# 288 instead of 320 columns of scores for a key block: a quarter of the own block shares columns with the far block

## The chip, the cores and the metric

One Trainium2 chip, and one of its cores. The metric is device microseconds of one execution. The kernel has five instruction streams: PE (matmuls, with the weight loads shown apart as PEld), ACT (exponentials and copies), DVE and POOL (elementwise work), and SP, which issues DMAs. Streams run in order and wait for each other by semaphores.

## The reference, cut to what matters

Four layers follow each other on `x` of 2048 tokens by 512 features, each with a layer norm ahead and a residual behind. Layers 1 and 3 are linear attention (`A`), layers 2 and 4 are attention in a sliding window (`B`). Both have 32 heads of 16 features.

```python
def _B_ref(x, wqkv, wo):
    H = 32; Dh = D // H; W = 256
    q, k, v = ...                       # x @ wqkv, split in heads
    scores = jnp.einsum("bhqd,bhkd->bhqk", q, k) * (Dh ** -0.5)
    mask = (idx[:, None] - idx[None, :] >= 0) & (idx[:, None] - idx[None, :] < W)
    p = _softmax(jnp.where(mask, scores, -1e9), axis=-1)
    return heads_joined(einsum("bhqk,bhkd->bhqd", p, v)) @ wo
x = x + _A_ref(_layernorm(x), A_wqkv, A_wo)
x = x + _B_ref(_layernorm(x), B_wqkv, B_wo)
x = x + _A_ref(_layernorm(x), A_wqkv, A_wo)
x = x + _B_ref(_layernorm(x), B_wqkv, B_wo)
```

A key k is seen by the 256 queries k to k + 255. A block of 64 keys is therefore seen by 320 queries: its own 64 (where the query must not be before the key), 192 that see all its keys, and 64 far ones (where the query must be less than 256 behind the key). A query offset r of the own part sees keys up to r; the far query with the same offset sees keys above r. So together the two parts hold 64 queries' worth of scores in 128 columns.

## The kernel before

**Tiles.** Tokens come in 16 tiles (or blocks) of 128, numbered j; half-blocks b of 64 keys. `kB` holds keys with two heads side by side: 64 keys by 2 heads are 128 columns of weights, and 32 rows are two heads of 16 features. A scores matmul so has 32 rows and gives 128 partitions (key, head) by queries; four of them, one for each row group gq, run in the 32x128 tile shape of PE into four PSUM banks. f counts four groups of eight heads, of which one operation takes two (fs).

**Near scores** (`b_scores`, operations "s", "ex", "mk"). For each j, b and fs: 8 matmuls of 256 queries (L599), two exponentials of 1024 columns on ACT (L609, each on two banks, out of PSUM into the slot P of block j), and on DVE one multiplication of the own 64 columns with a 0/1 triangle, `tri[0]` (L615, 512 elements). So four "s", eight "ex" and four "mk" a block; the last two blocks are cut short by the end of the sequence.

**Far scores** (`b_far`, "sF", "exF" and "mf" below). For each j up to 13: 32 matmuls of 64 queries (L632), two exponentials of 1024 columns (L641), and two masks of 1024 elements (mf), on DVE (L650) or POOL (L649).

**Values** (`b_values`, "pv"). For each j and half h, 2 x 24 matmuls of 34 columns, with 128 columns of P as weights (L674), over six half-blocks of j-2, j-1 and j; then a reciprocal (L685) and a multiplication (L686) on DVE. P has three slots in layer 2 and four in layer 4. So the exponentials of block j + 1 in layer 2 overwrite the slot of block j - 2 and wait for the pv of block j; the far part of block j is first read by pv of block j + 2.

**Around it.** While blocks of a B layer run, tiles of its front are made (aout, norm, transposes, bq, bk, bv with their copies bqe, bke, bve out of PSUM on ACT or DVE), and behind it bout, res, the next norm and, after layer 2, the keys and queries of layer 3 with their exponentials E (L392). The norm goes DVE stats (L330), POOL ve and rs (L332, L333), DVE xn (L334). `tok` (L369) and `feat` (L383) are helpers that record the 512-column and 128-column matmuls of many steps under one line.

**Order.** The graph of 2532 operations is placed by a packed table: for each operation its place in one list, its engine among those allowed, and for each PSUM tile its bank. `place` only reads it; `synchronise` then sets the semaphore waits that the dependences need. Each engine plays its share of the list in order.

```python
order = [ops[raw[2 * k] + 256 * raw[2 * k + 1]] for k in range(n)]
o.eng = ("PE", "ACT", "DVE", "POOL", "SP")[raw[2 * n + o.i]]
x.banks = [raw[3 * n + k]]
```

Of the kernel before, what the change touches and what calls it, by code (L numbers as in the profile page):

```python
# [9 lines left out]
ALU = mybir.AluOpType  # L10
# [202 lines left out]
class Plan:  # L213
# [372 lines left out]
    def b_scores(self, j, b, fs, key):  # L586
# [3 lines left out]
        q = P * j + 64 * b  # L590
        ns = min(256, S - q)
        last = (q + ns - 1) // P

# [11 lines left out]
        out = lambda h, m, w: bass_view(K.P(sl)[:, h, fs[0], 384 * b:384 * b + w], [[2816, m], [704, n], [1, w]])  # L605
        for h in range(2):
            def ex(e, h=h):
                i = bass_view(K.PS[:, ps[2 * h].banks[0], :], [[512, 2], [ns, n], [1, ns]])
                return e.activation(out(2 * h, 2, ns), i, ACT.Exp, bias=0.0, scale=0.25)  # L609

            self.on("ACT", "ex", ex, key + 0.01 * h, act(2 * ns * n), wr=[("P", sl, f, b, h) for f in fs], rd=[("P", sl, f) for f in fs], ps=[ps[2 * h], ps[2 * h + 1]])

        def mk(e):
            x = out(0, 4, 64)
            return e.tensor_tensor(x, x, K.tri[:, 0, :].unsqueeze(1).unsqueeze(1).to_broadcast([P, 4, n, 64]), ALU.mult)  # L615
# [3 lines left out]
    def b_far(self, j, key):  # L619

        K = self
        ps = [Tile(1, "S") for _ in range(4)]

        def put(e):
            m = None
            for f in range(4):
                for b in range(2):
                    q = P * j + 64 * b + 256
                    for gq in range(4):
                        rows = slice(32 * gq, 32 * gq + 32)  # L630
                        c = 128 * f + 64 * b
                        m = e.matmul(K.ps(ps[gq])[:, c:c + 64], K.kB[rows, j % 4, 2 * f + b, :, :], K.XQ[rows, f, q:q + 64], start=True, stop=True, tile_position=(32 * gq, 0))  # L632
            return m

        self.pe("s", put, key, 1, 512, mode=(32, 128), occ=245, rd=[("kB", j % 4, 0), ("kB", j % 4, 1), ("XQ", j + 2)], ps=ps)
        sl = j % self.rp
        far = lambda h: bass_view(K.P(sl)[:, 2 * h, 0, 256:320], [[704, 8], [384, 2], [1, 64]])
        for h in range(2):
            def ex(e, h=h):
                i = bass_view(K.PS[:, ps[2 * h].banks[0], :], [[128, 8], [64, 2], [1, 64]])  # L640
                return e.activation(far(h), i, ACT.Exp, bias=0.0, scale=0.25)  # L641

            self.on("ACT", "ex", ex, key + 0.01 * h, act(1024), wr=[("F", sl, h)], rd=[("P", sl, 0)], ps=[ps[2 * h], ps[2 * h + 1]])

        for b in range(2):
# [6 lines left out]
            engs = {"DVE": dve(1024, "2x")}  # L652
            if K.par["gp"]:
                engs["POOL"] = (1260, 1320)
            else:
                mk = lambda e, mk=mk: mk(e, "DVE")
            self.g.add("mf", engs, mk, key + 0.02 + 0.01 * b, rd=[("F", sl, 0), ("F", sl, 1), ("tri",)], wr=[("F", sl, b, 1)])

    def b_values(self, j, h, key):
# [6 lines left out]
        for f in (2 * h, 2 * h + 1):  # L666
            def put(e, f=f):
                m = None
                for gq in range(4):
                    r = 4 * f + gq  # L670
                    u = 4 * (f - 2 * h) + gq
                    for i, (b, c) in enumerate(blocks):
                        o = 384 * (b % 2) + c
                        m = e.matmul(K.ps(ps)[:, 34 * u:34 * u + 34], K.P((b // 2) % rp)[:, gq, f, o:o + P], K.vB[:, (b // 2) % 4, b % 2, r, :], start=i == 0, stop=i == len(blocks) - 1)  # L674
                return m
# [22 lines left out]
    def b_last(self, j, key):  # L698
# [4 lines left out]
        for h in range(2):  # L703
# [9 lines left out]
            self.copy("oTe", ps, lambda h=h: K.oT[:, s, h::2, :], lambda ps=ps: K.bf(ps, 256).rearrange("p (c n) -> p c n", c=2), key - 0.14 + 0.1 * h, 256, wr=[("oT", s, h)])  # L713
# [19 lines left out]
    def middle(self, ph):  # L733
# [25 lines left out]
        for j in range(T):  # L759
# [4 lines left out]
            wide = [2, 2]  # L764
            for f in range(4):
                for b in range(2):
                    if f % wide[b] == 0:
                        self.b_scores(j, b, list(range(f, f + wide[b])), base + j + (f + b) / 4)
                if f % 2:
                    h = f // 2  # L770
                    self.b_values(j, h, base + j + (h + 1) / 2 + par["k_pv"])
            if j + 2 < T:
                self.b_far(j, base + j + par["k_far"])
# [22 lines left out]
    r"c-rk(1Jq?nlFo<>WR`8)wr$(CZQHhO+qP|2wQYCpd+)ER>6z)7?d|Q|b9PU~|G&KV2EL5=B3_<%jfrF;8#GZ(6a&T@Hqi{3=q9BR6T`$bsZ44U",  # L796
    r"%cL=}O&pWf#5L)Rnmi_+NpJF+_@=$dVDg##CZkDUI+#JGqse3{nyIFk>0}C+X(qENXq-uCN}435kntv|8Emqc#wMKEX_}bCX1SSenwo4TndxkX",
    r"m>Fh;X=b{ZT_(IaZL*uLCWk3yikrgbuIXlSn&zgv*=_EbnI@6xVa}LbW|qlnhMJY;7gNr(Fsn>YGt8VdtIcq8-?TKn%tvO88DYws(xxPwGb7C?",
    r"6B&w_*=CO!ZO)rH=2w&4d~7b52d0l1W9FK@rnebuJ~1!NJ~PjJYSx;EX1-ZxN|<q`j7bXX%_FnGj5h{0n9s~YlMFVRYUXou(PW29X1^(GqQGU7",
    r"!W=N0%@vaz4w_OB6|S1crZhY;Dd3O+Xbgu<4TG@BJT*tmQIis)!58M4Nd>u0eRJJBHx*13^QCEJu9+9+D^tmof#_i2YZC)<Kuz<FA!uzFaza^n",  # L800
    r"$FwoIpd1J^fp1M)lN(ZlLLHL_(m*>?*QAB-jDrZKDWrqSCOyQ2dL|b1HMLD_=x5?Ud8lRjo48N`JWPa&kQWA+d=MWhK~Xc%#Do0M$Yg{JP#Gqe",
    r"MP{)n01Zq*SYir6LsJ+gnn`A<X$F&EnW+jbpbFH5de9MS!(_9?R5w#h9jI!ynodw3wwVUd5E{XD(;1GL=FkOpn3m8Ux<M;w3+<pQw1(rR4RnAT",
    r"=7i}1lVJ*UhovwTmcdDL2ByKg<}56SZE({}hf`(-yl1w<Ot@uMz${n^=U_Ihg73|0m;*bYC%kVKz#7;IYhfWAhudZm?1Emf8&1F;SPXOFB-}Cc",
    r"Afo9FKbXBRAI?J`*attFjnEG^!8-WBEP<cQX1D--;Ua{CQ*a4BH0vQ8{%peIWe5-b;R;m12rvK+!3H=C5g`I@fk$uzDq<vf0!Lv#RKf#r8XiML",
    r"{1C3fRyYVB!$)uzjzJ`>jFIskM8Rut1*771xDTH~G`xzR!&A5cpFkD73D@v5cnDST8C1htFbN;P3#g8h@eX_e@o@@1hZL9quVX5Vj_*JXjDZO;",
    r"B__d`*bozAGQ5F}a4O!0FJT}w#-un62f@4W6*R@^7z<}$226yhF*e@BjF=p6;d_t?;$SAs4DZ8COoLy;Ec^hnKwA6;vfyAyhjlP3WX1IO6V%0Q",
    r"P!qFZW^9J_uogDK7ML9uV{Kf5&G9yN!ljr4?_g)li7oMG$c0_-7s!pRups^lv#~YK!I$t9+u&UM7M`KOt{4vizlXbs_#ETnJ^T(VcEkHP4+(qV",
    r"4=^7KVO#8udGJRljP)@eR)Zqg0INe@EQ;;0J=TB)xB_cJ0w{((u{f^64p;ygYk}ZO?1%}W1S+n<)z}O3<610<z0qMQT!#;^5B9}Gum#uSVBCO-",
    r"VJmLKB(M=ZF2jeo376w$e1t<_JC??wPzIyfvKZYChY?T?ci=E60y{B=9fIX?DDJ|dFbs>qhZxh=wjbectYc%@;TYTQ!H+SH9f8GRFV?jq@mm~)",
    r"`*4AcYrn@55YH~O`|&%hXWzx-_9%XW@8Kdl8sEo$xY$0mi*Skk0Y}18`wrH(&ujxb3I<?*Y-q<|3LD>kfXi%3`y~#<WB4^bw}bFFCa_=O2|R#}",  # L810
    r"?5B7TM?+(~+<t?fVM2QdGuY4ZG5&}zY({$+U*Jjn2{YLz_ywl1@7SMlEWT?O;xCxij>98pZF74HGu!ca8gtn9Y&zS*PQcW5BA&sVHkD0p6WRA|",
    r"V%yT@vU%)T%wm(+y!ISswfSsEo6R<{*=;AA+cvfNE!k$av+ZixcC!Vn*e<raJ&$TH;IG)jUc`bnnSF_uu#LTpZLP6|th0S>Ve4%>8_t%r8*P6J",
    r"c9ZRA2U@i4ZFt+$4zerk0K3`tvV-k5o7DEUrR;V)#73~CZ6CYCma)6+P}{+lwY%*a`++TIciOeKyxn6f*dlhF9cGK#y>_J?ZY$bi_K+Q6E7?`{",
    r"h>d7V*wr?Y9cK^QG4Q1=ZpT7o`<2~lCqOFt+HSF_X*{&D<KURBY+KtX_JmDCRcusS)sD2s?T5CSU2m(~kL(6J+NP!Pc7jbuAKRlgJ)N@??I@dp",
    r"+EWM0NEhrR`-#m&pW2i5yxnIf+p%_vooe^nj`W%R$zHNw*aP;IJ!pTno#?dv#eQec*ex{8cBb#`S-X|G(69Eg%}rzMHu}NlAxn8F8%?)NUFk=g",
    r"ox0IWOLWoZpl__wb~4nR9POaYw3C25Wg(<p^tlx(Kw0UE{ni$ut2P|Xum$OwooS2Ebvw(3r=oPj&bBvg1e#-S*<w_IBGNY$i3(Fi>P^L|58bwv",
    r"s0`h)ed${&OC{(#ia{l*GL@t6X(;ue;gpZcQ&0MVO3{y$pLSCf8b&`+Y3fB)X(UynyS6%wrV(_{)}@~*CXJ$46q)YZ*ffB0QWSb%2hu}(l=e_m",
    r"8brq^4o#)wRF4MJ7@9_LDH_G2TvVSP+4wY_hENT9Y!gsTicSe>u5Cc`Y%MxK4XHmJr1`cEO{9L*hz`+Mnnb_Q6FZI?(+rwSP3RPjr@b_RPSX@h",
    r"MEmFrC8qs!j*?JQnn`Er0yU$gG>ekadAdcj3HT(<q1%Lfkrq*H61IGYu95Nyx<Sq9E;(*N*Xa^nrj~S*!gDKHOjjr(U!^6~nj&yyUP||98Aav$",
    r"w4Czs3W~xHXeGtwhm@Zq@pFp9tLRrMz%MB-&!yF5I62Luc$|WwaU1eHpHfnMK0<9N0WYMpe3;tNIZnur=mjkx=Ew97CE{?rhTf$ow3dk9qxX3o",  # L820
    r"CFc(~I<Kdc{60OS4RoGUa18!{I&n<?kUr$%9E(5V#9We}(#M>HOK@RM%}Kc+cjjbVgwyaf?!wo(D3{{${1I)W3j8q@<4shWEAnP4!-Y5%-{8tz",
    r"mM?H6uFB>3BH!dHe2IJWE$+kB_!GL#pHg4$&T08G>c>6#bNYnS@fXyCKjrjXoj>Cm+>0~taPG?e`Ewr0HTer3z#}*#*Wye(m<MtL&dguZARfx2",
    r"_$$i7mw5<(O<8#<U*Y9k!w%zRT${V`3a)9davdJcb$JXo<gr}KHsXa`pU3fH9?xI$B5ustxE^QcCY*ztGRQ`5#$WMf&dJSr32$PQuek-U<=p%Y",
    r"uj7`yh4b)w{+1_jUf#eHITugj?|3VJ&y#r@ujC*2N1no~cq(t_X}p75@oH|*cX&Fl;TilB-{pI}ldUwD`@D-E@NVA2E#x8Z<<|U&_i-DZ$1}MD",
    r"&*#UypWE^QCOOE5cow(g!#tax@DYB>3z+37pW<UYhv)KfKF!a#BR}U8e3D=A8GeV~<@fk!ZYFspkNm>L<X0{t;ib4lkfQRE3rPtv5>Z47O96=_",
    r"`6RNGl>DMnN(zdT($Z2|Nf~J^V`ZGglr~aUdP^T^E90e|#FF;XSC&W==^*{2qb!w9;w7r|mkBaJVoNs}D9fa~Oq9+tNG3@S2`7VPvUHK2GDPA?",
# [187 lines left out]
```

## Time and profile before

| | us |
|---|---|
| three timed runs | 431.07, 431.77, 432.0 (median 431.77) |
| profiled execution, first to last instruction (span) | 428.2 |
| what lies around the span (median less span) | 3.57 |
| first exponential of layer 2, last end of one | 69.0, 235.0 |
| first exponential of layer 4, last end of one | 269.7, 419.3 |

| engine | busy us | share of the span |
|---|---|---|
| PE | 392.7 | 92% |
| PEld | 257.9 | 60% |
| DVE | 356.2 | 83% |
| ACT | 347.4 | 81% |
| POOL | 128.6 | 30% |

The profiled execution's own time is taken as its span with the 3.57 us around it, which is the median of the runs. A line such as `L609 ACT ACTIVATE pb<-ps` is a group of instructions of line 609 on ACT that writes pb and reads ps. Busy time of PE is a union of modelled intervals: a matmul of 64 columns shows 0.19 us, though the next starts 0.03 us later. Instructions that follow each other at once on ACT or DVE overlap by about 0.1 us, so their spacing is shorter than their duration. The granted clock of PE is 1.00 up to 400 us.

### The profile page before, as it was taken

To read this page: it belongs to the slowest core of one execution; us is meant where nothing else is said; L and a number is where in the kernel's file an instruction comes from. 1 tells how busy PE (TensorE), PEld (TensorE's weight loads), DVE (VectorE), ACT (ScalarE), POOL (GpSimd) and SP (SyncE) were. 2 spreads that over 40 slices of the span, in tenths; PEclk is the share of its full clock that TensorE was granted. 3 is DMA by queue.
4 is the path that set the end of the run, shared out by engine and by line. 5 is a ranking of instruction groups with operands and counts; after the bars stand their busy time and mean duration, and the time that the engine had idled before them with its cause. 6 is when DMAs were issued, how large, how long until landed. Compare 5 with 4: busy or idle time off the path is not lost.

```text
span 428.2 us, 17035 instructions
## 1 busy us (share of the span) xinstructions
PE 392.7 (92%) x7471; PEld 257.9 (60%) x7548; DVE 356.2 (83%) x796; ACT 347.4 (81%) x433; POOL 128.6 (30%) x223
## 2 busy tenths in 40 slices
PE   8899999999899999999999999999889979997775
PEld 3445676766465566565565768585657746765544
DVE  6998899998998799887887789998798699875564
ACT  2423547999899999999998164999999999999992
POOL 4789322101240233130503303212144324332000
PEclk9999999999999999999999999999999999999968
DMA  7933016432153533453324000452434522553222
GB/s 248 269 74 87 2 42 160 117 90 70 39 111 64 103 103 77 91 112 55 95 47 65 19 2 26 114 120 63 113 62 106 116 77 77 116 133 102 64 52 51
DMA packets 66978, 37.81 MB, mean 88 GB/s; under 512 B 48248, under 2 KB 61816, under 8 KB 66904
## 3 DMA queue, kind: packets, MB, share of 16 engines
q1 hardware_dynamic: 66176, 34.75, 34.7%
q0 software_dynamic: 720, 1.97, 1.3%
q8 instruction: 59, 0.97, 1.0%
q14 instruction: 15, 0.12, 0.1%
q10 hardware_dynamic: 8, 0.00, 0.0%
HBM read 6.29 MB, written 2.10 MB: 20 GB/s over the span
## 4 chain that ended last, share of the span: by engine, by line
PE 42%; ACT 35%; DVE 16%; issue 4%; DMA 3%; POOL 1%; POOLq 0%; ACTq 0%
ACT pb L609 23%; PE ps L369 14%; PE ps L383 11%; PE ps L674 7%; ACT pb L641 6%; PE ps L599 4%; ACT vp L609 3%; DVE stats L330 2%; DVE XQ L526 2%; DVE vp L394 2%; ACT tE L392 1%; DVE tE L393 1%; DVE vp L334 1%; DMA xT<-xn 1%; DVE xres L537 1%
## 5 line engine op out<-in xcount | busy, mean ns | idle before, releaser
L609 ACT ACTIVATE pb<-ps 128x1024 bf16<-128x1024 f32 (+2 forms) x224 | 207.0, 1039 | 7.5 <-PE ps L599 6.1
L674 PEld LDWEIGHTS ps<-vB,pb 128*128 128x128 bf16 x2560 | 78.0, 96 | 13.0 <-DVE pb L615 2.8
L674 PE MATMUL ps<-vB,pb 128*128 128x34 bf16 x2560 | 83.6, 178 | 2.0 <-DVE pb L615 1.1
L392 ACT ACTIVATE tE<-ps 128x512 bf16<-128x512 f32 x64 | 38.8, 609 | 41.0 <-PE ps L369 20.6
L383 PE MATMUL ps<-xT,wBp 128*128 128x128 bf16 x1024 | 69.5, 219 | 2.1 <-DMA xT<-xn 0.8
L332 POOL TENSOR_SCALAR ve<-mv 128x1 f32<-128x1 f32 x64 | 16.6, 260 | 174.0 <-DVE mv L331 172.4
L383 PEld LDWEIGHTS ps<-xT,wBp 128*128 128x128 bf16 x1024 | 58.9, 98 | 14.8 <-issue 3.6
L615 DVE TENSOR_TENSOR pb<-pb,tri 128x512 bf16<-128x512 bf16 x112 | 48.0, 436 | 12.3 <-ACT pb L609 11.6
L599 PE MATMUL ps<-XQ,kB 32*128 32x256 bf16 (+2 forms) x1024 | 50.1, 270 | 6.9 <-ACT pb L609 3.4
L641 ACT ACTIVATE pb<-ps 128x1024 bf16<-128x1024 f32 x50 | 49.4, 1061 | 1.1 <-PE ps L632 1.0
L369 PE MATMUL ps<-wA,XQ 128*128 128x512 bf16 x177 | 46.3, 380 | 3.6 <-DVE vp L394 0.7
L537 DVE TENSOR_TENSOR xres<-ps,xres 128x512 bf16<-128x512 f32 x63 | 43.0, 685 | 7.3 <-PE ps L369 6.4
L649 POOL TENSOR_SCALAR_AFFINE_SELECT pb<-pb 128x1024 bf16<-128x1024 bf16 x30 | 35.3, 1175 | 38.5 <-ACT pb L641 37.3
L330 DVE BATCH_NORM_STATS2 stats<-xres 128x6 f32<-128x512 bf16 x64 | 43.1, 680 | 2.6 <-DMA xres<-in_A_x_dram 2.0
L333 POOL TENSOR_TENSOR rs<-ve,negh 128x1 f32<-128x1 f32 x64 | 37.5, 586 | 5.3
L383 PE MATMUL ps<-XQ,wA 128*128 128x128 bf16 x512 | 36.1, 219 | 0.4 <-DVE vp L394 0.2
L599 PEld LDWEIGHTS ps<-XQ,kB 32*128 32x128 bf16 x1024 | 15.5, 92 | 33.8 <-ACT pb L609 14.9
L369 PE MATMUL ps<-M,XQ 128*128 128x512 bf16 x115 | 31.7, 381 | 4.0 <-DVE XQ L526 1.6
L383 PEld LDWEIGHTS ps<-XQ,wA 128*128 128x128 bf16 x512 | 30.6, 98 | 7.7 <-DVE vp L394 1.2
L369 PE MATMUL ps<-wBo,oT 128*128 128x512 bf16 x104 | 30.1, 395 | 3.4 <-ACT pb L609 0.9
L369 PE MATMUL ps<-wBv,xT 128*128 128x512 bf16 x106 | 30.7, 381 | 2.7 <-issue 0.8
L369 PEld LDWEIGHTS ps<-wA,XQ 128*128 128x128 bf16 x192 | 16.1, 98 | 21.5 <-ACT XQ L353 1.7
(109 smaller groups left out, 541.2 us busy)
## 6 DMA issues: line engine op xcount, KB each, us to landing
vB<-vS SPq DMA_DIRECT2D x64, 136.0 KB, 2.5
kB<-vp SPq DMA_DIRECT2D x64, 128.0 KB, 2.2
out_dram<-xres POOLq DMA_DIRECT2D x15, 128.0 KB, 2.3
wA<-in_A_wqkv_dram SPq DMA_DIRECT2D x3, 512.0 KB, 5.9
xres<-in_A_x_dram SPq DMA_DIRECT2D x2, 512.0 KB, 4.9
pb<-in_B_wqkv_dram SPq DMA_DIRECT2D x1, 1024.0 KB, 9.0
xres<-in_A_x_dram SPq DMA_DIRECT2D x3, 256.0 KB, 4.9
wAo<-in_A_wo_dram SPq DMA_DIRECT2D x1, 512.0 KB, 7.4
```

The lines of the kernel that those rows point to most:

```text
L330: self.on("DVE", "stats", lambda e: e.bn_stats(K.stats[:, t, :], K.xres[:, t, :]), key, dve(512), rd=[("xres", t)], wr=[("stats", t)])
L333: self.pow = self.on("POOL", "pow", lambda e: e.tensor_tensor(K.rs[:, t, :], K.ve[:, t, :], K.negh[:], ALU.pow), key + 0.03, (640, 690), r ...
L369: m = e.matmul(K.ps(ps), lhs(c), rhs(c), start=c == 0, stop=c == 3)
L383: m = e.matmul(K.ps(ps)[:, f * P:(f + 1) * P], w(c, f), xT(c), start=c == 0, stop=c == 3)
L392: self.on("ACT", "E", lambda e: e.activation(K.tE[:, s, :], K.ps(ps), ACT.Exp, bias=0.0), key, act(512), wr=[("tE", s)], ps=[ps])
L537: self.on("DVE", "res", lambda e: e.tensor_tensor(K.xres[:, t, :], K.ps(po), K.xres[:, t, :], ALU.add), key, dve(512), rd=[("xres", t)], w ...
L599: m = e.matmul(K.ps(ps[gq])[:, ns * i:ns * i + ns], K.kB[rows, j % 4, 2 * f + b, :, :], K.XQ[rows, f, q:q + ns], start=True, stop=True, ti ...
L609: return e.activation(out(2 * h, 2, ns), i, ACT.Exp, bias=0.0, scale=0.25)
L615: return e.tensor_tensor(x, x, K.tri[:, 0, :].unsqueeze(1).unsqueeze(1).to_broadcast([P, 4, n, 64]), ALU.mult)
L641: return e.activation(far(h), i, ACT.Exp, bias=0.0, scale=0.25)
L649: return e.affine_select(out=x, in_=x, compare_op=ALU.is_ge, fill=0.0, base=-2, pattern=[[0, 16], [-2, 64]], channel_multiplier=1)
L674: m = e.matmul(K.ps(ps)[:, 34 * u:34 * u + 34], K.P((b // 2) % rp)[:, gq, f, o:o + P], K.vB[:, (b // 2) % 4, b % 2, r, :], start=i == 0, s ...
```

## The change

The far and the own part of a half-block share columns for a quarter of it. Near scores now begin at query 32 of the block (224 queries for 256). The far operation computes 128 partitions by 64 columns as before, but its two halves of 64 partitions (32 keys by 2 heads) get different queries: the upper keys the far queries 0 to 63, the lower keys the far queries 0 to 31 and then the own queries 0 to 31. For that each 32x128 matmul becomes two 32x64 ones with their own weight loads. The own mask (mk) takes its first 32 columns out of the far part (columns 288 to 319 of P) and its other 32 from where they were, and writes both to the own 64 columns; the far mask (mf) then clears what isn't far. So mk now reads what both far exponentials wrote, mf waits for the masks that read its columns, and the far operation of block j comes ahead of the values of block j. Blocks 14 and 15 keep the old form. In P, heads are laid out in another order, and the two banks of an exponential need no longer be neighbours.

The table is new as a whole. Unpacked, with the operations of the two versions set against each other, it has 41 far masks on POOL and 15 on DVE (35 and 21 before). In layer 2, ACT has 6 more bqe and one more each of bke, bve and oTe, and 2 fewer ve (the copies of values for layer 3); in layer 4, 3 more bve, one more Te (a transpose's copy) and 2 fewer bke; DVE has them the other way round. On ACT the two far exponentials of a block stand between its exponentials of f = 0, 1 and of f = 2, 3 in most blocks. Before, they were mostly those of one or two blocks earlier, in layer 4 also of the same block. Block 7 of layer 2 is an example, from its far exponentials to the first exponential of block 8:

```
ACT: exF0 exF1, ex(f2b0), bqe, ex(f2b0), bke, E, ex(f2b1) x2 | ex of block 8, f0b0
DVE: mk(f0b1), xn, xn, mk(f0b0)
PE:  pv(h0), aout x2, s of block 8, f0b0
```

```diff
 def b_scores(self, j, b, fs, key):
         ps = [Tile(1, "S") for _ in range(4)]
-        q = P * j + 64 * b
-        ns = min(256, S - q)
+        skip = 32 if j + 2 < T else 0
+        q = P * j + 64 * b + skip
+        ns = min(256 - skip, S - q)
         last = (q + ns - 1) // P
+        span = lambda two, free: bass_view(K.PS[:, two[0].banks[0], :], free([512 * (two[1].banks[0] - two[0].banks[0]), 2]))
...
-        out = lambda h, m, w: bass_view(K.P(sl)[:, h, fs[0], 384 * b:384 * b + w], [[2816, m], [704, n], [1, w]])
+        out = lambda h, w: bass_view(K.P(sl)[:, fs[0], h, 384 * b + skip:384 * b + skip + w], [[1408, 2 * n], [1, w]])
...
+        if skip:
+            return
...
 def b_far(self, j, key):
-                    q = P * j + 64 * b + 256
+                    q = P * j + 64 * b
+                    c = 128 * f + 64 * b
                     for gq in range(4):
                         rows = slice(32 * gq, 32 * gq + 32)
-                        c = 128 * f + 64 * b
-                        m = e.matmul(K.ps(ps[gq])[:, c:c + 64], K.kB[rows, j % 4, 2 * f + b, :, :], K.XQ[rows, f, q:q + 64], start=True, stop=True, tile_position=(32 * gq, 0))
+                        x = K.XQ[rows, f, q + 256:q + 320]
+                        for half in range(2):
+                            m = e.matmul(K.ps(ps[gq])[64 * half:64 * half + 64, c:c + 64], K.kB[rows, j % 4, 2 * f + b, 32 * half:32 * half + 32, :],
+                                         x if half else bass.AP(x.tensor, x.offset, [x.ap[0], [-256, 2], [1, 32]]), start=True, stop=True, tile_position=(32 * gq, 64 * half))
...
+        for fs in ((0, 1), (2, 3)):
+            for b in range(2):
+                def mk(e, b=b, fs=fs):
+                    x = bass_view(K.P(sl)[:, fs[0], 0, 384 * b + 288:384 * b + 320], [[704, 8], [-256, 2], [1, 32]])
+                    o = bass_view(K.P(sl)[:, fs[0], 0, 384 * b:384 * b + 64], [[704, 8], [32, 2], [1, 32]])
+                    t = K.tri[:, 0, :].rearrange("p (a n) -> p a n", a=2).unsqueeze(1).to_broadcast([P, 8, 2, 32])
+                    return e.tensor_tensor(o, x, t, ALU.mult)
+
+                self.on("DVE", "mk", mk, key + 0.02 + 0.01 * b + 0.2 * fs[0], dve(512, "2x"), rd=[("P", sl, f, b, h) for f in fs for h in range(2)] + [("F", sl, 0), ("F", sl, 1), ("tri",)],
+                        wr=[("P", sl, f, b, 2) for f in fs] + [("near", sl, b, fs[0])])
...
-            self.g.add("mf", engs, mk, key + 0.02 + 0.01 * b, rd=[("F", sl, 0), ("F", sl, 1), ("tri",)], wr=[("F", sl, b, 1)])
+            self.g.add("mf", engs, mk, key + 1.5 + 0.01 * b, rd=[("F", sl, 0), ("F", sl, 1), ("tri",), ("near", sl, b, 0), ("near", sl, b, 2)], wr=[("F", sl, b, 1)])
...
 def middle(self, ph):
-                if f % 2:
-                    h = f // 2
-                    self.b_values(j, h, base + j + (h + 1) / 2 + par["k_pv"])
             if j + 2 < T:
-                self.b_far(j, base + j + par["k_far"])
+                self.b_far(j, base + j + 0.8)
+            for h in range(2):
+                self.b_values(j, h, base + j + (h + 1) / 2 + par["k_pv"])
...
-TABLE = (the packed order of before)
+TABLE = (the packed order of after)
```

## The prediction

> **What bounds the kernel now.** I read four views in turn: busy time in stretches, the chain of waits, the groups by line and form, and the timeline of single stretches. The first exponential of layer 2 starts at 69.0 us and its last ends at 235; those of layer 4 run from 269.7 to 419.3. Columns: stretch, length, busy us of each engine.
>
> ```profile
> 70.00:235.00 165.00, 155.10 (x3147) 100.35 (x3178) 144.12 (x330) 156.79 (x189) 41.46 (x68) 1.00 0.38 84
> 268.00:420.00 152.00, 136.98 (x3089) 92.98 (x3115) 119.13 (x259) 146.71 (x170) 40.29 (x57) 0.97 0.39 94
> ```
>
> The fourth of the busy columns is ACT: 95% of layer 2, 97% of layer 4. PE shows 94% and 90% (too high, since matmul ends are modelled and overlap), DVE 87% and 78%. So layer 4 has one limit, layer 2 has a limit with two engines close behind. The chain of waits says the same, for each of the two stretches and in its longest pieces:
>
> ```profile
> by line: ACT pb L609 25.8%; PE ps L369 16.6%; PE ps L674 12.3%; PE ps L383 8.4%; ACT pb L641 7.5%; PE ps L599 6.7%; issue 2.7%; ACT tE L392 2.3%; DVE XQ L526 2.2%; DMA oT<-o 2.2%; DVE pb L615 1.6%; DVE stats L330 1.2%; DVE vp L394 1.2%; DVE
> by line: ACT pb L609 37.2%; PE ps L369 9.1%; PE ps L383 8.6%; ACT vp L609 8.5%; ACT pb L641 7.9%; issue 6.6%; PE ps L674 5.6%; PE ps L599 3.9%; DMA xT<-xn 3.3%; ACT vp L641 2.5%; DVE XQ L526 2.1%; DVE xres L537 1.6%; DVE o L686 1.1%; PE ps
> ...
> 358.62 12.83 ACT pb L609 x14
> 391.65 13.54 ACT pb L609 x15
> ```
>
> L609 is on the chain for 25.8% of 165 us (42.6 us) in layer 2 and 45.7% of 152 us (69.5 us) in layer 4.
>
> **Exponentials: fewer columns.** Fifteen back to back take 13.54 us, 0.903 us apiece. The tail holds a smaller form:
>
> ```profile
> 410.93 1.51 ACT L609 ACTIVATE pb<-ps 128x768 bf16<-128x768 f32 x2
> 412.31 1.04 ACT L641 ACTIVATE pb<-ps 128x1024 bf16<-128x1024 f32 x1
> ```
>
> Two of 768 columns go from 410.93 to 412.31, 0.69 apiece; so a column costs (0.903-0.69)/256 = 0.83 ns. The change cuts 1024 to 896 in 8 exponentials of each of 14 blocks of 2 layers: 224 x 128 x 0.83 ns = 23.9 us off ACT. The far exponentials keep 1024 columns. Runs per instruction stay 4 (near) and 16 (far), so the new axis order I cost at nothing.
>
> **Engines reassigned by the new table.** In layer 2 ACT takes over 6 bqe, 1 bke, 1 bve, 1 oTe and gives up 2 ve; in layer 4 it takes 3 bve and 1 Te and gives up 2 bke. With 0.48 us for a 512-column copy (0.61 for bke; row means 607 and 769 ns less the 0.13 to 0.16 by which neighbours overlap) that is +3.3 and +0.9 us. Net, ACT loses 8.7 us in layer 2 and 11.0 in layer 4, 19.7 in all: the ceiling of the gain. DVE loses about 9 copies and 6 far masks (mf), which go to POOL: roughly 9 us less, off the chain. POOL has room: its ve row waits 172.4 us for work.
>
> **Scores matmuls.** L599 streams 224 columns for 256: eight in 0.40 us are two sets of four, 0.11 us apart, so 13 ns a set, 2 sets, 112 operations: 3.0 us less PE.
>
> **Far matmuls.** They go from 32 in 32x128 tiles to 64 in 32x64 tiles, with twice the weight loads. Nearest rows:
>
> ```profile
> 120.45 0.41 PE L632 MATMUL ps<-XQ,kB 32*128 32x64 bf16 x32
> 79.80 0.40 PE L506 MATMUL ps<-XQ,zs 128*32 128x128 bf16 x16
> 120.86 1.37 PE L674 MATMUL ps<-vB,pb 128*128 128x34 bf16 x48
> ```
>
> One matmul lasts 0.19, so the 32 far ones start within 0.22 us: eight sets of four, 29 ns a set. L506 shows column tiles side by side: sixteen start within 0.18 us, four sets, though 16 in sequence would need 16 x 0.055. If row and column tiles combine, 64 still take eight sets, 0.22 us; if the two halves follow each other, 0.46; if nothing overlapped, L674's 25 ns apiece makes 1.6. I take 0.30, nearest to L506: +0.08 x 28 = +2.2 us of PE, with 0 and +6.7 as ends and +39 as the far end (a gain would need more than eight tiles at once, and there are eight). With the scores that is -0.8: PE is unchanged.
> [...]
> Switches between tile shapes stay about as many (332 before, 339 after, counted along PE's order); a gap of 89 to 92 ns shows at each, +0.6 us.
>
> **Masks.** The four own-block masks (mk) keep 512 elements, now in runs of 32, half of them fetched from column 288. The row is L615, 436 ns; whether runs cost is bounded by L358's CASTs, 689 ns in runs of 16 against 685: nothing. The other end is a full-rate pass, L537's 685 ns: 112 x 0.25 = +28 us of DVE. I take nothing; a gain has no row that would bring it.
>
> **What the move makes wait.** The masks move from behind their own exponentials to behind both far ones. On DVE phi, res and stats queue behind the mask; for it wait the values matmuls (pv), behind them on PE the next block's scores, and in layer 2, with three P slots, the next block's exponentials, which overwrite what pv reads. On POOL and DVE mf waits for the masks too, ve and rs queue behind it, and xn for those; only pv two blocks later needs it, so I cost it at nothing while POOL idles; else 1.2 us apiece.
> Block 7 of layer 2 by its new order: between the far exponentials and the first of block 8, ACT has four exponentials (4 x 0.80), a bqe, a bke and an E (0.61 + 0.77 + 0.61): 5.2 us of cover. Meanwhile DVE does two masks and two xn (4 x 0.44), PE pv (1.37), one aout (1.04) and the scores (0.40): 4.6 us. Margin 0.6 us. Before, the masks started two far exponentials earlier, 1.8 us more. So the move costs nothing if the other waits there stay under 0.6.
>
> **Sum.** Along the old chain alone: 42.6/0.917 = 46 exponentials of layer 2 and, without the 11 us of blocks 14 and 15, 58.5/0.917 = 64 of layer 4, at 0.107 each: 4.9 + 6.8 = 11.7 us. The ceiling is 19.7. Where ACT steps back, PE's pieces (L369, L674, L383) are next, above all in layer 2. I take 6 there and 8 in layer 4, 14 in all. Span 428.2 - 14.0 = 414.2; the median of the runs, 431.77, lies 3.57 above the span, which I keep: 417.8.
>
> **Rivals.**
> *PE takes over in layer 2.* For it: PE's four lines hold 44% of that chain, and PE is busy 94%. Against: that share is overstated by the overlapping ends. Then only layer 4 pays: 431.8 - 8 = 423.8. Masks at full rate end there too: DVE grows by 14 a layer, to 144 - 7 + 14 = 151 us in layer 2, past ACT's 148.
> *The masks' new place closes a loop (slower).* For it: 0.6 us of margin, three slots, DVE at 87%. Against: chains of this sort show ACT waiting for L599 only 6.1 us in all. Each microsecond of overshoot costs 14 in layer 2, layer 4 having a fourth slot; it decides from 14/14 = 1.0 us. At 1.5: 417.8 + 21 = 438.8.
> *The tiles don't do what they promise.* At 1.6 us a far operation PE gains 19 us a layer: 155 + 19 and 137 + 19 are 9 and 4 us over today's stretches, 445. L506 speaks against it.
>
> **How the numbers follow.** Likeliest 0.57 (its own range 410 to 422: ceiling 19.7, chain sum 11.7, both by 2 more for the reordered first layer), PE takes over 0.19, no change 0.04, loop 0.16, tiles 0.04. A measurement of this kernel tells 0.2%, 0.9 us, from no change. Faster is 0.57 + 0.19 = 0.76, same 0.04, slower 0.20. Below 409 I leave 0.04, above 435 some 0.15.
>
> **What would show it.** Right: L609 rows at 128x896, mean near 950 ns, back to back at 0.80; ACT busy about 20 us less with its share of both layers a little lower; L615's successor near 436 ns; far matmuls starting within 0.2 to 0.5 us; layer 4 shortened more than layer 2. Wrong: ACT idle before the exponentials, released by scores, up by over 10 us (loop); PE without gaps in layer 2 (PE takes over); far matmuls over 1 us; masks near 680 ns.

## The result, and the profile after

The changed kernel takes 426.71 us (median of four runs, 426.09 to 427.46) against 431.42 (four runs, 430.95 to 432.0): a ratio of 0.9889, 95% interval 0.9863 to 0.9915. That is 4.7 us less, where 14.0 were forecast. A later set of runs of the same kernel (after_again below, the repeat) gave 0.9883 [0.9858, 0.9908]. The profiled execution took 426.09 us for a span of 424.4. In every run since, the time lies 1.7 to 2.0 us above the span. By that the profiled execution of the kernel before, with its span of 428.2, took some 430 us, about 1.5 less than the median, so differences of spans and layers against it may come out that much too small.

From the first to the last scores exponential, layer 2 went from 165.9 to 164.9 us and layer 4 from 149.6 to 147.4; layer 2 began 1.4 us earlier, and the stretch behind layer 4 grew by 1.1. In the repeat the layers took 165.4 and 145.1, so a layer of one and the same kernel differs by 0.5 to 2.3 us between two profiled executions; the layers below are each from one execution.

The page of the changed kernel, busy time by engine and then the engines on the chain that ended last, and below them the same chain of the kernel before:

```profile
PE 393.9 (93%) x8370; PEld 266.9 (63%) x8444; DVE 349.0 (82%) x785; ACT 330.6 (78%) x438; POOL 134.1 (32%) x229
...
PE 62%; ACT 20%; DVE 12%; issue 4%; DMA 1%; SPq 0%; POOLq 0%; POOL 0%
```

```profile
PE 42%; ACT 35%; DVE 16%; issue 4%; DMA 3%; POOL 1%; POOLq 0%; ACTq 0%
```

ACT lost 16.8 us of busy time (19.7 were planned), and its share of the chain fell from 35% to 20%, while PE's rose from 42% to 62%. Two stretches laid on the two layers say the same (columns as in the prediction: PE, PEld, DVE, ACT, POOL, then the granted clock of PE, the DMA share and GB/s):

```profile
68.00:233.00 165.00, 157.46 (x3627) 106.57 (x3663) 142.83 (x326) 150.25 (x194) 46.44 (x75) 1.00 0.42 86
267.00:415.00 148.00, 136.93 (x3527) 95.84 (x3547) 113.98 (x256) 136.79 (x170) 42.66 (x60) 1.00 0.40 94
```

ACT fell from 156.8 to 150.3 of 165 us in layer 2, while PE rose. The granted clock, the third figure from the end, is a second difference: in layer 4 it was 0.97 before and is 1.00 here. In the kernel before it is at half for 9.7 us near the end of layer 4; from 400 to 410 us, the kernel before and then the repeat:

```profile
400.00:410.00 10.00, 7.57 (x198) 4.47 (x200) 5.24 (x14) 9.66 (x11) 0.54 (x1) 0.83 0.38 84
400.00:410.00 10.00, 9.32 (x225) 5.87 (x222) 8.26 (x21) 9.81 (x13) 0.00 (x0) 1.00 0.44 98
```

This goes with the table: in every profiled execution of the old order the clock of layer 4 is 0.93 to 0.98, in every one of the new order 1.00; layer 2 is at 1.00 in all. For PE, 9.7 us at half the clock are worth 4.9 us at most, as an estimate; no run here separates what they cost from the rest, so layer-4 figures are best compared within one order. The chain of waits of the same two stretches, by line:

```profile
by line: PE ps L369 23.1%; PE ps L688 17.5%; PE ps L383 13.7%; ACT pb L611 9.7%; PE ps L601 7.7%; ACT pb L649 5.9%; PE ps L639 4.8%; issue 3.4%; DVE xres L537 2.4%; DVE stats L330 1.8%; DVE pb L659 1.3%; ACT tE L392 1.1%; DVE tE L393 1.1%; 
by line: ACT pb L611 22.5%; PE ps L369 16.5%; PE ps L383 13.8%; PE ps L688 12.3%; PE ps L601 7.8%; ACT vp L611 6.9%; ACT pb L649 5.2%; PE ps L639 4.3%; issue 3.3%; ACT vp L649 2.0%; DVE xres L537 0.9%; DVE xn L334 0.9%; DVE stats L330 0.8%;
```

The near exponentials (L609, now L611) fell from 25.8% to 9.7% of the chain in layer 2 and from 45.7% to 29.4% (pb and vp) in layer 4. What came in their place are PE's own lines: projections (L369, L383), values (L688), scores (L601) and the far matmuls (L639), which were not among the lines shown before and now hold 4.8% and 4.3%. The groups by form (busy us, mean ns, idle before and its releaser):

```profile
L611 ACT ACTIVATE pb<-ps 128x896 bf16<-128x896 f32 x200 | 170.3, 933 | 11.6 <-PE ps L601 10.9
L659 DVE TENSOR_TENSOR pb<-pb,tri 128x512 bf16<-128x512 bf16 x100 | 41.0, 430 | 8.7 <-ACT pb L649 4.3 <-ACT pb L611 4.2
L639 PE MATMUL ps<-XQ,kB 32*64 32x64 bf16 x1792 | 19.8, 202 | 1.3 <-ACT pb L611 1.0
L639 PEld LDWEIGHTS ps<-XQ,kB 32*64 32x64 bf16 x1792 | 16.4, 102 | 7.9 <-ACT pb L611 4.2 <-DVE vp L555 0.8 <-DVE stats L330 0.6
```

The exponentials and the masks are what was forecast (933 and 430 ns). The third row is not: 28 far operations now occupy 19.8 us, 0.71 each, against 0.41 before. A last view, the waits (total us, times, longest): ACT now waits for the scores 14.4 us, 6.1 before, and DVE for the far exponentials 4.3.

```profile
ACT pb L611 <- PE ps L601: 14.4, 27, 1.2
DVE pb L659 <- ACT pb L649: 4.3, 3, 1.9
```

### The profile page after: what moved, and what is told of

It reads as the page before. It is cut to its first block, busy times and chain, and to the rows that moved or that the text cites. A ratio compares the mean times of both kernels' runs of the same rounds, so it can differ in the third digit from the quotient of the medians.

```text
span 424.4 us, 18880 instructions
## 1 busy us (share of the span) xinstructions
PE 393.9 (93%) x8370; PEld 266.9 (63%) x8444; DVE 349.0 (82%) x785; ACT 330.6 (78%) x438; POOL 134.1 (32%) x229
## 4 chain that ended last, share of the span: by engine, by line
PE 62%; ACT 20%; DVE 12%; issue 4%; DMA 1%; SPq 0%; POOLq 0%; POOL 0%
PE ps L369 21%; PE ps L383 14%; PE ps L688 12%; ACT pb L611 12%; PE ps L601 6%; ACT pb L649 4%; PE ps L639 3%; ACT vp L611 2%; PE ps L444 2%; DVE tE L393 1%; DVE xres L537 1%; DMA wA<-in_A_wqkv_dram 1%; DVE stats L330 1%; DVE XQ L394 1%; DVE vp L394 1%
## 5 line engine op out<-in xcount | busy, mean ns | idle before, releaser
L611 ACT ACTIVATE pb<-ps 128x896 bf16<-128x896 f32 (+3 forms) x224 | 187.2, 920 | 15.2 <-PE ps L601 14.4
L688 PE MATMUL ps<-vB,pb 128*128 128x34 bf16 x2560 | 83.6, 178 | 1.4 <-ACT pb L611 0.5
L688 PEld LDWEIGHTS ps<-vB,pb 128*128 128x128 bf16 x2560 | 77.5, 96 | 11.5 <-issue 5.1
L383 PE MATMUL ps<-xT,wBp 128*128 128x128 bf16 x1024 | 68.7, 219 | 0.9 <-issue 0.8
L383 PEld LDWEIGHTS ps<-xT,wBp 128*128 128x128 bf16 x1024 | 58.9, 98 | 10.9 <-issue 4.8
L392 ACT ACTIVATE tE<-ps 128x512 bf16<-128x512 f32 x64 | 37.6, 599 | 36.0 <-PE ps L369 21.3
L332 POOL TENSOR_SCALAR ve<-mv 128x1 f32<-128x1 f32 x64 | 15.5, 242 | 157.4 <-DVE mv L331 155.4
L667 POOL TENSOR_SCALAR_AFFINE_SELECT pb<-pb 128x1024 bf16<-128x1024 bf16 x36 | 42.0, 1166 | 68.4 <-DVE pb L659 66.8
L601 PE MATMUL ps<-XQ,kB 32*128 32x224 bf16 (+4 forms) x1024 | 46.8, 256 | 5.0 <-ACT pb L611 1.5
L649 ACT ACTIVATE pb<-ps 128x1024 bf16<-128x1024 f32 x50 | 48.5, 1024 | 3.4 <-PE ps L639 2.7
L369 PE MATMUL ps<-wA,XQ 128*128 128x512 bf16 x175 | 46.5, 385 | 4.8 <-DMA wA<-in_A_wqkv_dram 1.7
L659 DVE TENSOR_TENSOR pb<-pb,tri 128x512 bf16<-128x512 bf16 x100 | 41.0, 430 | 8.7 <-ACT pb L649 4.3
L601 PEld LDWEIGHTS ps<-XQ,kB 32*128 32x128 bf16 x1024 | 15.5, 92 | 36.1 <-ACT pb L611 15.1
L383 PE MATMUL ps<-XQ,wA 128*128 128x128 bf16 x512 | 34.1, 219 | 0.0
L383 PEld LDWEIGHTS ps<-XQ,wA 128*128 128x128 bf16 x512 | 29.9, 98 | 5.5 <-issue 0.6
L369 PE MATMUL ps<-M,XQ 128*128 128x512 bf16 x113 | 29.5, 380 | 3.1 <-DVE rc L699 0.7
L369 PE MATMUL ps<-wBv,xT 128*128 128x512 bf16 x112 | 30.8, 380 | 1.6 <-issue 1.0
L369 PE MATMUL ps<-wBo,oT 128*128 128x512 bf16 x102 | 28.8, 383 | 3.0 <-issue 1.2
L369 PEld LDWEIGHTS ps<-wA,XQ 128*128 128x128 bf16 x192 | 17.0, 99 | 22.0 <-issue 5.4
```

The costliest lines, as they stand in the source:

```text
L369: m = e.matmul(K.ps(ps), lhs(c), rhs(c), start=c == 0, stop=c == 3)
L383: m = e.matmul(K.ps(ps)[:, f * P:(f + 1) * P], w(c, f), xT(c), start=c == 0, stop=c == 3)
L392: self.on("ACT", "E", lambda e: e.activation(K.tE[:, s, :], K.ps(ps), ACT.Exp, bias=0.0), key, act(512), wr=[("tE", s)], ps=[ps])
L601: m = e.matmul(K.ps(ps[gq])[:, ns * i:ns * i + ns], K.kB[rows, j % 4, 2 * f + b, :, :], K.XQ[rows, f, q:q + ns], start=True, stop=True, ti ...
L611: return e.activation(out(h, ns).rearrange("p (f g) c -> p f g c", f=n), i, ACT.Exp, bias=0.0, scale=0.25)
L649: return e.activation(o.rearrange("p (f g) b c -> p f g b c", g=2), i, ACT.Exp, bias=0.0, scale=0.25)
```

## The experiments

Two theories stood against each other. One, the instructions: the far operation costs PE far more than was forecast, and PE is full, so that its price goes through to the end. The other, the order: the new table and the masks' wait for both far exponentials take the gain back. Ratios are to the kernel before on the same chip; a hundredth of the ratio is 4.3 us. A difference between two such kernels is known to 2 to 3 us either way (their two intervals, added in squares). Some kernels leave work out; the diff, the text or the expectation says which. Cuts in the diffs are marked by three dots.

### The parts one at a time, in the new order

e6_order_alone keeps the new table and its waits, but computes near and far scores as before, and its own masks read their own columns:

```diff
-        q = P * j + 64 * b + skip
-        ns = min(256 - skip, S - q)
+        q = P * j + 64 * b
+        ns = min(256, S - q)
...
-        out = lambda h, w: bass_view(K.P(sl)[:, fs[0], h, 384 * b + skip:384 * b + skip + w], ...)
+        out = lambda h, w: bass_view(K.P(sl)[:, fs[0], h, 384 * b:384 * b + w], ...)
...
-                        x = K.XQ[rows, f, q + 256:q + 320]
-                        for half in range(2):
-                            m = e.matmul(K.ps(ps[gq])[64 * half:64 * half + 64, c:c + 64], ...)
+                        m = e.matmul(K.ps(ps[gq])[:, c:c + 64], K.kB[rows, j % 4, 2 * f + b, :, :], K.XQ[rows, f, q + 256:q + 320], ..., tile_position=(32 * gq, 0))
...
-                    x = bass_view(K.P(sl)[:, fs[0], 0, 384 * b + 288:384 * b + 320], [[704, 8], [-256, 2], [1, 32]])
-                    o = bass_view(K.P(sl)[:, fs[0], 0, 384 * b:384 * b + 64], [[704, 8], [32, 2], [1, 32]])
+                    o = x = bass_view(K.P(sl)[:, fs[0], 0, 384 * b:384 * b + 64], [[704, 8], [32, 2], [1, 32]])
```

> The work of before (256 near queries, far scores in 32x128 tiles, masks of the own columns in place) in the new order with the new waits. Theory A: the order by itself is neutral, 429 to 433 us. Theory B: the order costs, 437 us or more.

Measured: 434.28 us, 1.0057 [1.0036, 1.0079]. The new table by itself costs 2.5 us, between the two expectations. Its layers are 170.8 and 149.6 us: layer 2 is 4.9 longer than before. In it ACT is busy 2.6 us more (160.3 for 157.7; the table gives it more copies) and idle 2.3 us more (10.5 for 8.2).

e1_far_plain is the changed kernel with the far matmuls alone put back, 32 in 32x128 tiles (the third part of the diff above; the own queries 0 to 31 of the lower keys are left out):

> The changed kernel with its order, cut and masks, but the far scores as 32 matmuls in 32x128 tiles (as before); the own queries 0 to 31 of the lower keys are left out, far scores stand in their place. Theory A (PE became the limit: it holds 62% of the chain after, and a far operation now spreads its starts over 0.50 us instead of 0.23, 7.6 us of PE in all): two thirds of that comes back, 421 to 423 us. Theory B (the new order and its waits cost what the cut brings; PE is only carried along): no change from 426.7, within 1 us.

Measured: 418.99 us, 0.9683 [0.9631, 0.9734]; layers 164.0 and 141.5. This is faster than either theory had it. From e6 to e1 the shorter exponentials and scores bring 3.7 hundredths, 16.1 us. From e1 to the changed kernel the 64 matmuls take 2.1 hundredths back, 8.9 us.

e2_no_cut is the changed kernel with 256 near queries again (the first two parts of the diff above), the far matmuls in their 64 tiles:

> The changed kernel with near scores and exponentials of 256 queries again (ACT +23.9 us, PE +3.0 us), all else as changed. Theory A: ACT has slack, only PE's 3 us and a little more show: 428 to 431 us. Theory B: the cut is worth its full 12 to 20 us and the order hides it: 437 us or more.

Measured: 438.49 us, 1.0131 [1.0067, 1.0194]. Here the 64 matmuls cost 3.2 us over e6, against 8.9 where the exponentials are short. The pages fit that: the chain of e6, then of e2, then of e1, by engine.

```profile
ACT 46%; PE 40%; DVE 9%; DMA 2%; issue 2%; SPq 0%; POOLq 0%; POOL 0%; DVEq 0%
```

```profile
ACT 45%; PE 43%; DVE 7%; issue 2%; DMA 1%; SPq 0%; POOLq 0%; POOL 0%
```

```profile
PE 55%; ACT 22%; DVE 15%; DMA 4%; issue 2%; SPq 1%; POOLq 0%; POOL 0%; DVEq 0%
```

With 256 columns the chain runs over ACT as much as over PE; once they are cut it runs over PE. That this is why the price differs is a reading, and the old order, next, speaks against it as a rule.

So the whole change is +2.5 for the order, -16.1 for the cut and +8.9 for the far matmuls, -4.7 us. By way of e2 it is +2.5, +3.2 for the far matmuls and -10.4 for the cut: the two parts are not independent.

### The same parts in the old order

e3_cut_alone takes the kernel before and cuts near scores and exponentials to 224 queries (the own queries 0 to 31 are left out); e3b_columns_in_old takes it and splits each far matmul in two 32x64 ones, with the same queries for both halves:

```diff
-                        m = e.matmul(K.ps(ps[gq])[:, c:c + 64], K.kB[rows, j % 4, 2 * f + b, :, :], K.XQ[rows, f, q:q + 64], ...)
+                        for half in range(2):
+                            m = e.matmul(K.ps(ps[gq])[64 * half:64 * half + 64, c:c + 64], K.kB[rows, j % 4, 2 * f + b, 32 * half:32 * half + 32, :], K.XQ[rows, f, q:q + 64], ..., tile_position=(32 * gq, 64 * half))
```

> The kernel before with its old order and old far scores, and only the near scores and exponentials cut to 224 queries (own queries 0 to 31 are left out; the columns hold ones). Theory A: PE stands close behind ACT in any order, so the cut alone brings about 5 us: 425 to 428 us. Theory B: without the new order the cut brings the forecast 12 to 14 us: 417 to 420 us.

> The kernel before, only with each far matmul split in two 32x64 ones (same result): PE +7.6 us, ACT and order unchanged. If PE's price counts in full in the old order too: 438 to 440 us. If ACT is the limit there and hides it, as the forecast had it: 432 to 434 us. From the 4.2 us between e2_no_cut and e6_order_alone I expect between: 435 to 437 us.

Measured: 426.72 us, 0.9869 [0.982, 0.9918], for the cut; 439.62 us, 1.0201 [1.0146, 1.0255], for the split. The split costs 8.7 us in this order too, though the exponentials have 256 columns: 435 to 437 us were expected, and 439.62 lies in the range named for a price that counts in full. Its layers are 169.6 and 156.6 us, 3.7 and 7.0 longer (in layer 4 the granted clock was 0.95, 0.97 before). So a chain shared with ACT does not make the split cheap. The cut brings only 5.7 here, a third of what it brings in the new order. By layers, e3 has 162.7 and 147.9 us and e1 164.0 and 141.5. In layer 2, at the same clock, the two orders thus end close together with the cut, and the new one starts from a longer layer; they part in layer 4, where the clock was 0.97 in e3 and 1.00 in e1.

### Is it the column tiles or the number of instructions?

In the changed kernel the 64 starts of a far operation span 497 ns (median of 28; 223 before). In 24 of the 28 the first 32 starts take 139 ns, eight at a time, the sets 52, 32 and 32 ns apart; then no matmul starts for 99 ns; then one follows each 8.3 ns. With each matmul goes a weight load, and one more load starts ahead of the break, which so comes after 65 instructions. Two kernels separate tile shape from count. e1d_128_instr_rows issues each of e1's 32 row-tiled matmuls twice; e1e_64_instr_columns has 32 matmuls of twice the columns in the 32x64 tiles (two groups f share the weights of the first, and all halves get the far queries, so half of the far scores and the own ones among them are not computed):

```diff
+                        for _ in range(2):
                             m = e.matmul(K.ps(ps[gq])[:, c:c + 64], K.kB[rows, j % 4, 2 * f + b, :, :], K.XQ[rows, f, q + 256:q + 320], ..., tile_position=(32 * gq, 0))
```

```diff
-                        x = K.XQ[rows, f, q + 256:q + 320]
+                        if f % 2:
+                            continue
+                        x = K.XQ[rows, f:f + 2, q + 256:q + 320]
                         for half in range(2):
...
```

> As e1_far_plain (no column tiles, far scores as in the kernel before; own queries 0 to 31 of the lower keys left out), but every far matmul is issued twice: 64 matmuls with 64 weight loads in 32x128 tiles. Theory S (supply: PE takes the first 64 instructions of a burst at the array's rate, then stands still for 0.1 us and gets one matmul with its load every 8.3 ns): the starts spread over 0.57 to 0.60 us, with a gap near 100 ns after the 32nd matmul; time 426 to 430 us. Theory C (the column tiles are slow by themselves): sixteen sets of four at 29 ns, 0.46 us without a gap; time 424 to 427 us.

> The changed kernel with its column tiles, but half as many far matmuls, each over 128 columns (the weights of f = 0 and 2 serve for f = 1 and 3 too, and all halves get the far queries, so the scores are others): 32 matmuls with 32 loads in 32x64 tiles. Theory S: 64 instructions fit, starts spread over about 0.2 us without a gap, time 418 to 421 us. Theory C: the gap or the slow pace stays, spread above 0.3 us, time 423 us or more.

Measured: 425.02 us, 0.9869 [0.9811, 0.9927], for the doubled rows; 419.63 us, 0.9741 [0.9704, 0.9777], for the few columns. The four make a table:

| far operation | 32x128 tiles | 32x64 tiles |
|---|---|---|
| 32 matmuls, 32 loads | 0.9683, starts span 224 ns | 0.9741, 215 ns |
| 64 matmuls, 64 loads | 0.9869, 535 ns | 0.9889, 497 ns |

The count costs 1.9 and 1.5 hundredths, the shape 0.6 and 0.2, inside the intervals. The right column is the clean comparison: the same tiles and the same columns in all, at half the matmuls and half the loads. In the left one the doubled matmuls also double the columns, which at e1's 29 ns a set of four would take 0.46 us by themselves (theory C), so less than 0.1 of e1d's 0.535 is left for a slower supply. One far operation of each in the timeline (start, duration, matmuls), in the order changed kernel, e1, e1d, e1e:

```profile
124.12 0.71 PE L639 MATMUL ps<-XQ,kB 32*64 32x64 bf16 x64
```

```profile
117.03 0.41 PE L637 MATMUL ps<-XQ,kB 32*128 32x64 bf16 x32
```

```profile
122.18 0.72 PE L638 MATMUL ps<-XQ,kB 32*128 32x64 bf16 x64
```

```profile
117.57 0.43 PE L643 MATMUL ps<-XQ,kB 32*64 32x128 bf16 x32
```

Each duration is the span of the starts and the 0.2 us of the last matmul: 0.7 for 64 of either shape, 0.4 for 32 of either. e1d has no break, where theory S had one: its first 32 starts take 234 ns because its sets are of four, mostly 29 ns apart, and from the 33rd on a matmul with its load comes each 9.4 ns (median), 38 for four. In both kernels the 33rd matmul starts about 240 ns after the first, and the rest come at 4.2 to 4.7 ns an instruction. The reading that fits both is that the first 64 or so instructions run as fast as their tiles allow, and what follows comes at a slower supply; a break shows only where the tiles are faster than that. Matmuls and loads were always doubled together, so which of the two sets the pace is open, and where the supply is limited no run here shows.

### Do the masks wait too long?

e6b_order_no_wait is e6 with the own masks freed of the far exponentials:

```diff
-                self.on("DVE", "mk", mk, ..., rd=[("P", sl, f, b, h) for f in fs for h in range(2)] + [("F", sl, 0), ("F", sl, 1), ("tri",)],
+                self.on("DVE", "mk", mk, ..., rd=[("P", sl, f, b, h) for f in fs for h in range(2)] + [("tri",)],
```

> As e6_order_alone (the work of before in the new order), but the masks of the own block, which there read only their own columns, no longer wait for the far exponentials. Theory W (the new wait makes the 2.6 us that e6_order_alone lost): 431 to 432.5 us. Theory O (the order does): within 0.8 us of 434.3.

Measured: 433.42 us, 1.0072 [1.0047, 1.0097], layers 171.0 and 149.6, as e6. The wait isn't what the order costs. What else in the table does, ACT's added copies among them, I did not isolate.

### Which engine sets the end?

Five kernels relieve one engine or load it, and one repeats the changed kernel. e9_act_only is the kernel before with the exponentials alone cut (ACT -23.9 us by the forecast's sum, -17.6 in busy time; the own queries 0 to 31 stay without exponential). e8_less_pv is the kernel before without the sixth half-block in the values, 16 of 96 matmuls a block (PE some -11 us, an estimate: 16 at the 25 ns of L674 in each of 28 blocks); e8a_less_pv_after is that in the changed kernel; e11_both is e9 and e8 together. e10_pe_only is the changed kernel with the near scores at 256 columns and the exponentials at 224 (PE +3 us, by the prediction's 13 ns a set). The edit of e8, e8a and e11 to the values:

```diff
-        blocks = [(b, c) for b, c in blocks if b >= 0]
+        blocks = [(b, c) for b, c in blocks if b >= 0 and c < 256]
```

> The kernel before with only the exponentials cut to 224 queries, the scores matmuls still 256 (own queries 0 to 31 left out, ones in their columns): ACT 23.9 us less, PE unchanged. If ACT is the limit: 12 us faster. If PE is: 0 to 3 us faster, the rest of the 4.9 us of e3_cut_alone being PE's 3.0.

> The kernel before without the values matmuls of the farthest half-block (16 of 96 in a block; the far scores are still made but not used): PE about 11 us less, ACT, DVE and order unchanged. If ACT is the limit of the kernel before, as the forecast read it: at most 3 us faster. If PE is: 8 to 12 us faster.

> The changed kernel with scores matmuls of 256 queries again (PE +3.0 us), exponentials as changed; same result. PE's price one to one: 3 us slower than the changed kernel; if PE has slack there: 0 to 1 us.

> The changed kernel once more, beside the three others of this call: 4 to 5.5 us faster than the kernel before.

> The changed kernel without the values matmuls of the farthest half-block (as e8_less_pv, PE about 11 us less). If PE is the limit after the change: 6 to 10 us faster than the changed kernel, 416 to 420 us, where the same relief brought the kernel before about 1 us. If a chain of waits through the far operation is, and not PE's load: at most 2 us, 424 us or more.

> The kernel before in its old order with both reliefs, e9_act_only's shorter exponentials and e8_less_pv's fewer values matmuls. Theory L (ACT and PE are limits together, so that either alone brings little): clearly more than the sum of the two alone (5.8 + 1.1), 11 to 16 us faster than before, 415 to 420 us. Otherwise the sum: 424 to 425 us.

Measured, with the layers of the profiled execution and, in them, the time in which ACT had no work (165.9 and 149.6 before, ACT idle 8.2 and 3.8), and the granted clock of layer 4 (0.97 before):

| kernel | us | ratio [95%] | layers, us | ACT idle, us | clock, layer 4 |
|---|---|---|---|---|---|
| e9_act_only | 425.23 | 0.9865 [0.9836, 0.9895] | 163.7, 146.8 | 15.2, 9.3 | 0.98 |
| e8_less_pv | 430.24 | 0.9974 [0.9948, 1.0001] | 164.3, 150.5 | 7.0, 5.0 | 0.93 |
| e11_both | 423.32 | 0.9811 [0.9781, 0.9841] | 160.9, 146.6 | 12.9, 10.0 | 0.95 |
| after_again | 425.77 | 0.9883 [0.9858, 0.9908] | 165.4, 145.1 | 14.8, 8.6 | 1.00 |
| e8a_less_pv_after | 420.19 | 0.9741 [0.9708, 0.9774] | 163.8, 143.2 | 13.6, 7.0 | 1.00 |
| e10_pe_only | 425.75 | 0.9882 [0.9855, 0.9909] | 166.7, 147.8 | 15.4, 10.6 | 1.00 |

The same relief of PE brings 1.1 us before the change, within its interval of nothing, and 6.1 after it (0.9883 to 0.9741). By layers the picture is weaker. In layer 2 it brings 1.6 us in both; the two part in layer 4, 0.9 longer before and 1.9 shorter after, and there e8 had the clock at half for 20.2 us, against 9.7 in the kernel before and none in the other two. So the totals fit a limit that moved to PE, but some of the difference may be the clock, and in layer 2 this pair does not show the move. The chains: e8, e9, then the repeat and e8a.

```profile
ACT 45%; PE 34%; DVE 14%; issue 3%; DMA 2%; POOL 1%; SPq 0%; POOLq 0%; ACTq 0%
```

```profile
PE 67%; DVE 13%; ACT 10%; DMA 5%; issue 3%; POOL 1%; SPq 0%; POOLq 0%; ACTq 0%
```

```profile
PE 66%; ACT 19%; DVE 9%; DMA 2%; issue 2%; SPq 0%; POOLq 0%; POOL 0%
```

```profile
PE 52%; ACT 27%; DVE 14%; issue 4%; DMA 1%; SPq 0%; POOLq 0%; POOL 0%
```

Take the columns from ACT and PE holds 67% of the chain (e9); take 11 us from PE and ACT leads with 45% to 34% (e8). In layer 2 of the kernel before, relief of ACT brings 2.2 us, of PE 1.6, of both 5.0. That is 1.2 more than the two added, as two limits would have it, but layers vary by as much.

Of e9 and of the repeat the trace holds every matmul, so PE's occupation can be counted from the starts: each matmul's distance to the next one, but no more than the spacing that its kind shows back to back (218 ns for 512 columns, 55 for 128, 25 for 34), plus the gap, up to 95 ns, at a change of tile shape. PE so is occupied, as an estimate, for some 155 of 163.7 us in layer 2 of e9 (95%) and some 159 of 165.4 in that of the changed kernel (96%).

Three limits of this. e11 brings 8.1 us, little over the 6.9 of e9 and e8 added and short of the 11 to 16 expected of two limits; what holds it then is open (in its layer 2 of 160.9 us ACT is busy for 148.0 and DVE for 144.2). The clock of layer 4 was lower in e8 and in e11 than before, so these two may be too long there. And e10 misses its expectation: no change of the total where 3 us of PE were added to a full PE. Its layers are 4.0 us longer than the repeat's together, but its layer 2 began 2.7 us earlier (65.9 for 68.7). That beginning lies between 65.7 and 71.2 us in all these profiles, which I can't explain.

No kernel here that computes the whole reference is faster than the changed one by more than the intervals.

## Why the prediction was wrong, point by point

The direction was right and 426.7 lies between the 409 and 435 of the last sentence on chances, but the gain is a third of the 14.0 us forecast. What is missing, 9.3 us, is about what the 64 far matmuls cost, 8.9: with plain ones e1 gains 13.7 us by its ratio. That the total of e1 comes so near the forecast is in part luck, since its layer 2 does not (below).

**Exponentials and copies: right.** L611 has a mean of 933 ns (near 950 was forecast), and back to back 0.81 to 0.85 us (0.80 forecast), as the changed kernel's chain in layer 4 shows (start, length):

```profile
391.81 5.68 ACT pb L611 x7
400.39 7.62 ACT pb L611 x9
```

Seven take 5.68 us and nine 7.62. ACT's busy time fell by 7.1 and 9.0 us over the layers (8.7 and 11.0 forecast, somewhat too much).

**Far matmuls: the step that failed.** "I take 0.30, nearest to L506: +0.08 x 28 = +2.2 us of PE". Measured: starts spanning 0.497 us, so 0.274 x 28 = +7.7 us, beyond even the 0.46 of the upper end and far from 1.6; and 8.9 us of the whole time between e1 and the changed kernel. The row chosen as nearest, L506, has 16 matmuls, and the row before has 32: neither issues more than 64 instructions, and the longer row shown, L674, has 25 ns between its matmuls, so it could not show a supply of one in 8. The tiles did do what they promise: the first 32 start eight at a time, 32 to 52 ns a set. Their loads of 64 columns keep up with that: in the first four sets those of one tile start 28 to 31 ns apart, and e1e, with such loads in the same tiles but half as many, takes 0.215 us.

**"With the scores that is -0.8: PE is unchanged": failed with it.** It is 7.7 less 3.0, +4.7 us on PE.

**"That share is overstated": the second failed step.** The prediction set PE's 94% in layer 2 aside because modelled ends overlap. Counted from starts in e9, which has the matmuls of the kernel before, PE is occupied for some 155 us, 94% of the 165.9 before: the share was not overstated. So layer 2 gave some 2 us, not 6: e9 shows 2.2, e3 3.2, e1 1.9 against the kernel before. That PE's fullness alone holds layer 2 there is argued and not shown, since e8a took some 5.6 us of PE out of it (half of the estimate of 11) and gained 1.6. The rival "PE takes over in layer 2" told this mechanism, and its 423.8 us lies nearest to the 426.7, by luck in part: it had layer 4 pay 8 us and PE unchanged.

**Layer 4: right without the far matmuls.** 8 us were forecast; e1 has 149.6 - 141.5 = 8.1, against the kernel before and against e6 alike (e6 and e1 both at a clock of 1.00). With the 64 matmuls 2.2 remain (4.5 in the repeat).

**Masks: right.** 430 ns in runs of 32. The loop did not close: DVE waits for the far exponentials 4.3 us in three waits, and without that wait the order is no faster (e6b). The far masks wait on POOL 66.8 us for the own ones, and nothing on the chain follows from it.

**The order: not in the sum.** The copies that it moves to ACT were, at +3.3 and +0.9 us; its waits were costed at nothing, and e6 shows +2.5 us in all, +4.9 in layer 2. The granted clock of layer 4, 0.97 before and 1.00 with the new table, was not in it either. Why the cut is worth 16.1 us in the new order and 5.7 in the old stays open. That each list was made for its own durations of exponentials is one reading, the clock of layer 4 another, and neither was tried.

**"3.57 above the span, which I keep".** In every later run it is 1.7 to 2.0: the median was set against the span of a faster execution. The gain of 14.0 does not rest on it.

## What to carry to other kernels

Before work is moved off the engine that bounds a stage, count from the starts how full the next engine is; a busy share near 95% is not to be waved off because ends are modelled. Splitting matmuls into smaller tiles that run side by side cost here by the number of instructions, not by the columns (0.497 us for 64 matmuls and 64 loads, 0.215 for 32 and 32 with as many columns in all): count matmuls and loads of one burst, and look for a burst of that length in the trace before taking the pitch of a shorter one. A saving and a cost are worth measuring apart and together: the same 64 matmuls cost 3.2, 8.7 and 8.9 us in three surroundings, and the first two both had the long exponentials. And before layers of two tables are compared, look at the granted clock of each.

## What the runs showed of the hardware

In the changed kernel's bursts of 64 matmuls with 64 loads in 32x64 tiles (L639), the first 32 matmuls of 64 columns start within 139 ns; the 33rd comes 238 ns after the first, and from there on a matmul with its load takes 8.3 ns (9.4 in the 32x128 tiles of e1d). Eight tiles of 32x64 ran side by side there, the sets 32 to 52 ns apart, their loads of 64 columns 28 to 31. A mask whose operands run in pieces of 32 elements, half of them fetched 288 columns away, took 430 ns for 512 elements (L659), as the one in pieces of 64 did in the kernel before (L615, 436).
